# Part B's weights: three quarters of one Wo piece held in a PSUM bank, with three small banks and a new order of a segment

## The chip, the cores and the metric

The kernel runs on one core of a Trainium2 chip. The metric is the time of one execution on the device, in microseconds (us); a profile of one more execution comes with it. The engines that matter are TensorE (PE, matmuls; PEld its weight loads), VectorE (DVE), ScalarE (ACT), GpSimd (POOL), SyncE (SP, which issues most transfers) and the 16 DMA engines that carry them.

## What is computed

Two independent parts write the left and the right half of the output's columns. Part A is a sliding-window attention with dilation; the change does not touch it. Part B is a recurrent attention over segments of 32 rows with 8 memory rows that each segment hands to the next:

```python
for s in range(n_seg):                       # 64 segments of 32 rows, Dm = 640, H = 32, Dh = 192, M = 8
    h = jnp.concatenate([mem, xs], axis=1)   # 40 rows
    q = jnp.einsum('btd,dhe->bhte', h, Wq)   # Wq, Wk, Wv: 640 x 6144; Wo: 6144 x 640
    k = jnp.einsum('btd,dhe->bhte', h, Wk)
    v = jnp.einsum('btd,dhe->bhte', h, Wv)
    scores = jnp.where(mask, jnp.einsum('bhqe,bhke->bhqk', q, k) * scale, -1e9)
    o = jnp.einsum('bhqk,bhke->bhqe', softmax(scores), v)
    o = jnp.einsum('bhte,hed->btd', o, Wo)
    mem = o[:, :M, :]
    outs.append(o[:, M:, :])
```

So every segment needs all four weights, bf16, 7.9 MB each, and they do not all fit on the chip.

## The kernel before

**Pieces.** Wq, Wk and Wv are each cut into 4 groups g (eight heads) of 5 pieces dc, 128 x 1536 bf16 (384 KB); Wo into 24 pieces of 128 x 1280 (320 KB). Most pieces stay in SBUF (wres_...). Those in STREAMED (line 285) are copied to DRAM in a packed form (wcopy_...) while part A runs, and are fetched anew in every segment: 8 of Wk, 10 of Wv and 5 of Wo (8, 12, 17, 19, 23). `fetch` (line 472) takes a buffer of a ring of seven (`wstream`, tile t) and issues the load on SP (line 475). SP runs ahead of PE as far as the ring allows: a fetch waits until PE has finished with the piece that held the buffer seven pieces earlier.

**A segment** is a list of steps, ORDER (line 298; FIRST for segment 0), which fixes the order of the instructions on PE, DVE, ACT and SP. `q.g`, `k.g`, `v.g` are the projections of a group (line 562): 20 matmuls for the 24 new and 8 memory rows, and 20 more where the group's late rows are computed anew (RENEW: one group of k and one of v in each segment). The "late" rows are the last 8 rows of a segment, whose projections were made up to four segments ahead. `e.` copies a projection out of PSUM (line 601, or 568 for the late rows) and `T.` turns it in blocks on DVE (line 572); the tiles QT and KT are single, so the copy for the next group waits until the scores `S.` (line 626) have read them. Softmax is `sb`, `mx`, `sub`, `send` (lines 632 to 658), in place in the PSUM bank of the scores, with the exponential on ACT. `tp` (line 665) turns the probabilities on PE and `PT` (lines 673, 676) spreads them; `ve` copies the values (lines 615, 617); `mix` (line 689) multiplies probabilities and values in two banks, and `ot` copies the result (line 697) to the single tile OT. `out.g.half` (line 714) multiplies OT with Wo in the bank Y; `part` and `join` (lines 721, 726) add Y's halves; `last` (line 740) does the last six pieces of Wo, and `close` (lines 748, 749) writes the memory rows of the next segment to HX and the output rows to XS. `ql` projects late rows of the next segment's q. EVACUATE, HEADS and SPREAD say which of ACT (S) and DVE (V) does a copy.

**Rows in and out.** XS holds a segment's output rows after `close`. SP stores them in four transfers (line 772), one at each step of STORE_AT, and loads the next segment's x into the same tile after `ve.2` (line 535); `tx` turns it. The load waits for the stores.

**PSUM** has eight banks: three for projections (`ps_acc`), four small ones for S, tp, mix and last (`ps_x`, tile px) and Y (`ps_y`). A new px tile takes a bank whose last user is done.

**Around the segments.** Part A runs for the first 171 us or so, with the packed copies, the resident weights and the copies of x beside it. Then the first seven fetches go out, the rest of the resident weights follow, and segment 0 begins. After segment 63, `project_late` multiplies the late rows of all segments with Wo once more, in eight sums in PSUM.

Of the kernel before, what the change touches and what calls it, by code (L numbers as in the profile page):

```python
# [7 lines left out]
FP32 = mybir.dt.float32  # L8
BF16 = mybir.dt.bfloat16
ALU = mybir.AluOpType  # L10
# [13 lines left out]
def part_a(ctx, tc, A_x, A_wqkv, A_wo, out, ident, emit_loads):  # L24
# [241 lines left out]
    with tc.manual_schedule(engines={mybir.EngineType.PE, mybir.EngineType.DVE, mybir.EngineType.Activation}):  # L266
# [4 lines left out]
        for b in range(-1, n_blk):  # L271
# [10 lines left out]

STREAMED = {"q": ((), (), (), ()), "k": ((1, 3), (1, 2), (0, 2), (1, 3)), "v": ((0, 1, 4), (2, 4), (0, 2, 4), (0, 2)),
            "o": (8, 12, 17, 19, 23)}
PARTS = {}
SLOT = 1536
RENEW = {0: ("k0", "v2"), 1: ("k1", "v3"), 2: ("k2", "v0"), 3: ("k3", "v1")}
BLOCKS = 16  # L290
FIRST = """
    q.0 e.q0 T.q0 k.0 e.k0 T.k0 q.1 S.0 sb.0 e.q1 T.q1 k.1 mx.0 sub.0 e.k1 T.k1 send.0 v.0 ve.0 S.1 sb.1
    q.2 e.q2 tp.0 PT.0 T.q2 k.2 e.k2 T.k2 mx.1 sub.1 mix.0 ot.0 v.1 ve.1 send.1 S.2 sb.2 out.0.0 out.0.1
    tp.1 mx.2 sub.2 PT.1 q.3 e.q3 T.q3 k.3 send.2 e.k3 T.k3 mix.1 ot.1 v.2 ve.2 tp.2 PT.2 out.1.0 S.3
    sb.3 mx.3 sub.3 out.1.1 mix.2 ot.2 send.3 v.3 ve.3 out.2.0 tp.3 PT.3 tx out.2.1 part mix.3 ot.3 join
    ql eql last close Tql
# [12 lines left out]
LEAD_IN = 114  # L309
HEAD = 10  # L310

# [8 lines left out]
def part_b(ctx, tc, B_x, B_mem0, B_Wq, B_Wk, B_Wv, B_Wo, out, ident, n_seg, pre, nbuf, mid):  # L320
# [7 lines left out]
    wo_v = B_Wo.rearrange("h e d -> (h e) d").rearrange("(i k p) d -> p i k d", p=128, k=2)  # L328

    def streamed(u):  # L330
        return u[1] in STREAMED["o"] if u[0] == "o" else u[2] in STREAMED[u[0]][u[1]]

    def pieces(m, g):
# [14 lines left out]
    def quarter_cols(u):  # L348
        return 320 if u[0] == "o" else 384
# [11 lines left out]
    def quarter(w, u, i):  # L361

        n = quarter_cols(u)
        if isinstance(w, tuple):
            now = PARTS[u]
            v = w[0][:, n * i:n * i + n] if i < now else w[1][:, n * (i - now):n * (i - now) + n]
            return v.rearrange("p (b c) -> p b c", b=2) if u[0] == "o" else v
        if u[0] == "o":
            return w[:, 640 * (i // 2):640 * (i // 2) + 640].rearrange("p (b g c) -> p g b c", b=2, g=2)[:, i % 2]
        return w[:, n * i:n * i + n]  # L370

    def stream_cols(u):
        return quarter_cols(u) * PARTS.get(u, 4)

    def kept_cols(u):
        return quarter_cols(u) * (4 - PARTS[u]) if u in PARTS else unit_cols(u)
# [3 lines left out]
    def copy_streamed():  # L380

        for m, g in need:
            for u in pieces(m, g):
                if u in PARTS:
# [65 lines left out]
    def pool(name, **kw):  # L450
        return ctx.enter_context(tc.tile_pool(name=name, reuse_waits="tile", **kw))
# [10 lines left out]
    one = pool("b_one", bufs=1)  # L462
    small = pool("b_small", bufs=2)
    ps_acc = pool("b_ps_acc", bufs=3, space=PSUM)
    ps_x = pool("b_ps_x", bufs=4, space=PSUM)
    ps_y = pool("b_ps_y", bufs=1, space=PSUM)
    respool2 = pool("b_res2", bufs=1)
    place_resident(respool2, resident[n_pre + len(early):])
    wait.update(resident[n_pre + len(early):])

    fetched = {}

    def fetch(u):
        t = wstream.tile([128, SLOT], BF16, tag="ws")
        nc.sync.dma_start(t[:, 0:stream_cols(u)], copied[u])
        return t[:, 0:stream_cols(u)]

    pending = []
# [65 lines left out]
    def bank():  # L544
        return ps_x.tile([128, 512], FP32, tag="x", name="px")
# [212 lines left out]
    def segment(s):  # L758
# [10 lines left out]
        def step(name, *at):  # L769
# [75 lines left out]
    def project_late():  # L845
# [140 lines left out]
```

## Time and profile before

| | |
|---|---|
| median of 3 executions | 1868.72 us (1862.43 to 1874.19) |
| the profiled execution's own time | 1872.4 us |
| its span, first to last instruction | 1870.6 us |
| start of segment 0 on PE | 173.3 us |
| end of segment 0's last operation, line 749 | 211.3 us |
| that of segment 63 | 1805.8 us |
| granted TensorE clock, mean | 0.99 |

The page gives for each engine its busy time, share of the span and number of instructions, then the span in 40 equal slices, where a digit is a busy share in tenths. The DMA row is the mean busy share of the 16 DMA engines, the GB/s row what they moved. A row of the waits reads: engine and line that waited, what released it, us in total, times, the longest. A row by stretches gives the stretch, its length, the busy time of PE, PEld, DVE, ACT and POOL with their instruction counts, the granted clock, the DMA share and GB/s. In a row of instructions stand start, duration, engine, line, operation, output and inputs, count, and in brackets the idle time before it with what ended it. In a row of groups, the last part is total busy time, mean ns of one, and idle time before. "issue" is a wait that the profile does not explain.

### The profile page before, as it was taken

How to read it: one execution, taken by the hardware profiler on the slowest of the kernel's cores; microseconds unless marked ns; L12 is line 12 of the kernel's file. 1: busy time of each engine (PE TensorE's matmuls, PEld its weight loads, DVE VectorE, ACT ScalarE, POOL GpSimd, SP SyncE). 2: the span in 40 equal slices, each digit the busy share in tenths (PEclk: the TensorE clock that was granted, in tenths of full speed). 3: DMA queues.
4: the chain of work that ended last, by engine and by line, in shares of the span. 5: the costliest groups of instructions: out<-in, count | busy, mean ns of one | idle time of the engine just before them, and what ended most of it. 6: DMA issues, size and time to landing. Idle time of an engine off the chain costs nothing.

```text
span 1870.6 us, 91426 instructions
## 1 busy us (share of the span) xinstructions
PE 1651.0 (88%) x39286; PEld 1044.9 (56%) x39286; DVE 1289.4 (69%) x3671; ACT 683.2 (37%) x1821; POOL 548.6 (29%) x1612
## 2 busy tenths in 40 slices
PE   8898888888889888888888988888889888898888
PEld 5565555555555555555555555555555555555568
DVE  4786677667777776776777767777667777677740
ACT  3454333333333333333333333333333333333320
POOL 3001233233233233332333323323323333332320
PEclk9999999999999999999999999999999999999999
DMA  9926999999999999999999999999999999999991
GB/s 327 321 74 211 384 352 349 344 348 353 361 340 365 364 362 345 352 357 339 360 362 350 367 336 355 359 368 357 339 344 366 352 355 360 356 366 350 349 380 42
DMA packets 277859, 627.63 MB, mean 336 GB/s; under 512 B 64116, under 2 KB 76898, under 8 KB 277452
## 3 DMA queue, kind: packets, MB, share of 16 engines
q1 hardware_dynamic: 267020, 610.59, 91.4%
q0 software_dynamic: 10336, 11.12, 1.8%
q8 instruction: 308, 5.05, 1.1%
q14 instruction: 99, 0.81, 0.1%
q10 hardware_dynamic: 96, 0.06, 0.0%
HBM read 607.47 MB, written 22.91 MB: 337 GB/s over the span
## 4 chain that ended last, share of the span: by engine, by line
PE 48%; DMA 31%; DVE 10%; issue 5%; ACT 4%; SPq 1%; POOL 0%; ACTq 0%; DVEq 0%; POOLq 0%
PE acc L562 24%; DMA t<-wcopy_v 24%; PE Y L714 5%; DMA t<-wcopy_k 4%; PE px L626 3%; PE px L740 3%; PE pq L95 3%; PE px L689 3%; PE px L859 2%; DMA t<-wcopy_o 1%; PE po L161 1%; ACT OT L697 1%; ACT QT L721 1%; DVE OT L697 1%; PE px L665 1%
## 5 line engine op out<-in xcount | busy, mean ns | idle before, releaser
L562 PEld LDWEIGHTS <-HX 128*32 128x32 bf16 x19380 | 506.1, 97 | 385.7 <-issue 161.1
L562 PE MATMUL acc<-t,HX 128*32 128x384 bf16 x5812 | 433.8, 330 | 60.2 <-DMA t<-wcopy_v 38.8
L562 PE MATMUL acc<-wres_q,HX 128*32 128x384 bf16 x6460 | 327.5, 331 | 16.3 <-issue 14.7
L562 PE MATMUL acc<-wres_k,HX 128*32 128x384 bf16 x3876 | 269.7, 327 | 9.5 <-issue 8.4
L698 POOL COPY OL<-OT 128x96 bf16<-128x96 bf16 x256 | 158.9, 621 | 272.0 <-ACT OT L697 177.3
L562 PE MATMUL acc<-wres_v,HX 128*32 128x384 bf16 x3232 | 216.4, 330 | 5.1 <-issue 5.0
L697 DVE CAST OT<-px 128x240 bf16<-128x240 f32 x256 | 103.8, 405 | 164.0 <-PE px L689 148.4
L608 POOL COPY QT<-Lb 128x96 bf16<-128x96 bf16 x252 | 67.6, 268 | 479.2 <-PE px L626 478.9
L714 PE MATMUL Y<-wres_o,OT 128*32 128x320 bf16 x3840 | 189.9, 301 | 6.4 <-issue 6.4
L572 DVE STREAM_TRANSPOSE QT<-QT 128x384 bf16<-128x384 bf16 x256 | 146.6, 573 | 43.7 <-ACT QT L601 41.5
L697 ACT CAST OT<-px 128x240 bf16<-128x240 f32 x256 | 92.5, 361 | 222.9 <-PE px L689 131.3
L601 ACT CAST KT<-acc 128x384 bf16<-128x384 f32 x192 | 92.4, 481 | 223.1 <-PE px L626 174.0
L615 ACT CAST Vst<-acc 128x384 bf16<-128x384 f32 x256 | 123.5, 482 | 113.7 <-PE px L689 91.0
L626 PE MATMUL px<-KT,QT 64*64 64x40 bf16 (+1 forms) x4096 | 139.3, 189 | 28.2 <-DVE KT L572 20.6
L699 POOL DMA_DIRECT2D late_o<-OL x256 | 137.9, 539 | 77.0 <-POOL OL L698 60.5
L632 DVE SCALAR_TENSOR_TENSOR px<-px,mask 128x160 f32<-128x160 f32 x256 | 82.7, 323 | 108.3 <-PE px L626 107.7
L626 PEld LDWEIGHTS <-QT 64*64 64x64 bf16 (+1 forms) x4096 | 109.0, 109 | 86.2 <-issue 47.2
L714 PEld LDWEIGHTS <-OT 128*32 128x32 bf16 x4608 | 113.8, 96 | 58.5 <-issue 15.2
L572 DVE STREAM_TRANSPOSE KT<-KT 128x384 bf16<-128x384 bf16 x256 | 142.2, 556 | 3.1 <-ACT KT L601 1.5
L568 ACT CAST sb<-acc 128x384 bf16<-128x384 f32 x115 | 55.1, 479 | 232.7 <-PE acc L562 202.8
L644 ACT ACTIVATE px<-px 128x160 f32<-128x160 f32 x256 | 74.3, 290 | 145.1 <-DVE px L643 135.7
L689 PE MATMUL px<-PT,Vst 64*128 64x80 bf16 (+1 forms) x2048 | 122.6, 212 | 4.5 <-issue 2.5
(102 smaller groups left out, 2429.5 us busy)
## 6 DMA issues: line engine op xcount, KB each, us to landing
t<-wcopy_v SPq DMA_DIRECT2D x640, 384.0 KB, 5.9
t<-wcopy_k SPq DMA_DIRECT2D x512, 384.0 KB, 5.2
t<-wcopy_o SPq DMA_DIRECT2D x330, 320.0 KB, 6.0
wres_q<-in_B_Wq_dram SPq DMA_DIRECT2D x20, 384.0 KB, 8.0
late_o<-OL POOLq DMA_DIRECT2D x256, 24.0 KB, 5.2
wres_q<-late_o SPq DMA_DIRECT2D x16, 384.0 KB, 7.3
wres_o<-in_B_Wo_dram SPq DMA_DIRECT2D x19, 320.0 KB, 7.2
wres_k<-in_B_Wk_dram SPq DMA_DIRECT2D x12, 384.0 KB, 7.9
```

The lines of the kernel that those rows point to most:

```text
L562: nc.tensor.matmul(ps[n][32 * j:32 * j + 32].rearrange("p (f n) -> p f n", n=32), lhsT=X[:, dc, :], rhs=columns(w, (m, g, dc), j), start=( ...
L572: nc.vector.transpose(t, t)
L601: copies[1](columns_of(m, 0, 32), ps[-1][:].rearrange("p (f n) -> p f n", n=32))
L615: S_(Vst[:], ps[-1][:])
L626: nc.tensor.matmul(Sps[64 * h:64 * h + 64, a, :], lhsT=QT[k0:k1, L * f:L * f + 64], rhs=KT[k0:k1, f, :], start=(outer == 0 and a == 0), st ...
L632: nc.vector.scalar_tensor_tensor(out=Sps, in0=Sps, scalar=scale, in1=mask[:].unsqueeze(1).to_broadcast([128, 4, L]), op0=ALU.mult, op1=ALU ...
L644: nc.scalar.activation(t1[:], t1[:], ACTF.Exp)
L689: nc.tensor.matmul(ps[r][lo:hi, 2 * L * k:2 * L * k + 2 * L], lhsT=V[64 * r:64 * r + 64, col:col + hi - lo], rhs=PT[64 * r:64 * r + 64, 2 ...
L697: copy(OT[:, 6 * r:6 * r + 6].rearrange("p c n -> p (c n)"), ps[r][:, 0:6 * L])
L698: nc.gpsimd.tensor_copy(OL[:, g % 2].rearrange("p n c -> p c n"), OT[:, :, 32:L])
L699: nc.gpsimd.dma_start(late_o[s // 4][:, g, s % 4], OL[:, g % 2].rearrange("p n c -> p (n c)"))
L714: nc.tensor.matmul(Y[t:t + 32].rearrange("p (b c) -> p b c", b=2), lhsT=OT[:, slot(c), 0:32], rhs=quarter(w, ("o", i, 0), 2 * r + gv), sta ...
```

## The change

- STREAMED: in each segment 10 pieces of Wk, 8 of Wv and 4 whole ones of Wo are fetched.
- HELD: of piece 21 of Wo, three quarters (960 columns) are loaded once, at the start, and copied by DVE into a PSUM bank of their own (`hold`). The last quarter (320 columns, 640 bytes a partition) is packed in DRAM and fetched in each segment at the new step `w.0`; there ACT copies the 960 columns from PSUM into the same ring buffer beside it.
- `ps_x` has three banks in place of four. `project_late` takes its eighth sum from them after the first two blocks are stored.
- ORDER and FIRST are written anew. In ORDER, `send.1` stands ahead of `mix.0`, `k.2` between `S.0` and `S.1`, `out.1` ahead of `mix.2`, `v.3` behind `mix.2`, `w.0` between `tp.3` and `PT.3`.
- EVACUATE and HEADS: `e.q0` on ACT and `e.k3` on DVE for the current rows; both copies of `ot.2` on ACT.
- STORE_AT: the four stores are issued at `tp.0`, `mx.1`, `send.1` and `PT.0`, which puts two behind v.0's fetches and two behind v.1's. Five fetches stand between the last of them and the load of x, as before.

```diff
-STREAMED = {"q": ((), (), (), ()), "k": ((1, 3), (1, 2), (0, 2), (1, 3)), "v": ((0, 1, 4), (2, 4), (0, 2, 4), (0, 2)),
-            "o": (8, 12, 17, 19, 23)}
+STREAMED = {"q": ((), (), (), ()), "k": ((0, 3), (1, 2), (0, 2, 4), (1, 2, 4)), "v": ((0, 4), (3, 4), (1, 3), (2, 4)),
+            "o": (6, 11, 18, 22)}
+HELD = ("o", 21, 0)
...
 ORDER = """
-    q.0 e.q0 T.q0 k.0 k.1 e.k0 T.k0 q.1 S.0 sb.0 e.k1 e.q1 mx.0 sub.0 v.0 T.q1 ve.0 T.k1 q.2 S.1 send.0
-    e.q2 T.q2 sb.1 mx.1 k.2 tp.0 v.1 e.k2 q.3 PT.0 sub.1 mix.0 T.k2 send.1 tp.1 S.2 ve.1 ot.0 sb.2 e.q3
-    PT.1 mx.2 sub.2 k.3 T.q3 send.2 out.0.0 e.k3 v.2 out.0.1 mix.1 T.k3 S.3 ot.1 tp.2 sb.3 mx.3 v.3 PT.2
-    ve.2 mix.2 sub.3 out.1.0 send.3 out.1.1 ot.2 tp.3 ve.3 out.2.0 out.2.1 part tx PT.3 mix.3 ot.3 last
-    join ql close eql Tql
+    q.0 k.0 e.q0 T.q0 q.1 e.k0 T.k0 k.1 S.0 e.q1 sb.0 e.k1 T.q1 k.2 T.k1 mx.0 sub.0 S.1 e.k2 send.0 q.2
+    e.q2 sb.1 v.0 tp.0 mx.1 sub.1 ve.0 T.q2 v.1 send.1 T.k2 q.3 PT.0 mix.0 S.2 ve.1 ot.0 sb.2 e.q3 mx.2
+    tp.1 PT.1 k.3 mix.1 out.0.0 T.q3 v.2 out.0.1 e.k3 sub.2 T.k3 send.2 ot.1 ve.2 tp.2 S.3 PT.2 out.1.0
+    out.1.1 mix.2 sb.3 mx.3 sub.3 v.3 send.3 ot.2 tp.3 w.0 PT.3 out.2.0 out.2.1 ve.3 tx mix.3 part ot.3
+    join last ql close eql Tql
 """
-EVACUATE = {"k0": "SV", "k1": "SS", "k2": "VS", "k3": "SS", "q0": "VV", "q1": "SS", "q2": "SS", "q3": "VV"}
-HEADS = ("VS", "SV", "VS", "SV")
+EVACUATE = {"k0": "SV", "k1": "SS", "k2": "VS", "k3": "SV", "q0": "VS", "q1": "VS", "q2": "VS", "q3": "SV"}
+HEADS = ("VS", "SV", "SS", "SV")
-STORE_AT = ("tp.0", "PT.0", "tp.1", "e.k3")
+STORE_AT = ("tp.0", "mx.1", "send.1", "PT.0")
...
-    ps_x = pool("b_ps_x", bufs=4, space=PSUM)
+    ps_x = pool("b_ps_x", bufs=3, space=PSUM)
     ps_y = pool("b_ps_y", bufs=1, space=PSUM)
+    held = pool("b_ps_w", bufs=1, space=PSUM).tile([128, 512], FP32, name="held")
...
+    def hold():
+        t = wstream.tile([128, SLOT], BF16, tag="ws")
+        load_quarters(t[:, 0:960], HELD, (1, 2, 3))
+        nc.vector.tensor_scalar(out=held[:, 0:480].bitcast(mybir.dt.uint32), in0=t[:, 0:960].bitcast(mybir.dt.uint32),
+                                scalar1=0, scalar2=None, op0=ALU.bitwise_or)
+
     def fetch(u):
         t = wstream.tile([128, SLOT], BF16, tag="ws")
         nc.sync.dma_start(t[:, 0:stream_cols(u)], copied[u])
+        if u == HELD:
+            nc.scalar.copy(t[:, 320:1280], held[:, 0:480].bitcast(BF16))
+            return t[:, 0:1280]
...
+            elif name == "w":
+                fetched[HELD] = fetch(HELD)
...
-        sums = [bank()[:] for _ in range(4)] + [acc[0][:], acc[1][:], acc[2][:], y[:]]
+        sums = [bank()[:] for _ in range(3)] + [acc[0][:], acc[1][:], acc[2][:], y[:]]
...
+            else:
+                sums.append(bank()[:])
...
+    hold()
     fetch_first(nbuf)
```

FIRST gets `send.1` ahead of `mix.0`, `send.3` ahead of `mix.2` and `w.0` behind `tx`; the copies to DRAM take only the first quarter of the held piece.

More of the change, by code (lines that the diff above doesn't have):

```diff
@@ L292 @@
     q.0 e.q0 T.q0 k.0 e.k0 T.k0 q.1 S.0 sb.0 e.q1 T.q1 k.1 mx.0 sub.0 e.k1 T.k1 send.0 v.0 ve.0 S.1 sb.1
-    q.2 e.q2 tp.0 PT.0 T.q2 k.2 e.k2 T.k2 mx.1 sub.1 mix.0 ot.0 v.1 ve.1 send.1 S.2 sb.2 out.0.0 out.0.1
+    q.2 e.q2 tp.0 PT.0 T.q2 k.2 e.k2 T.k2 mx.1 sub.1 send.1 mix.0 ot.0 v.1 ve.1 S.2 sb.2 out.0.0 out.0.1
     tp.1 mx.2 sub.2 PT.1 q.3 e.q3 T.q3 k.3 send.2 e.k3 T.k3 mix.1 ot.1 v.2 ve.2 tp.2 PT.2 out.1.0 S.3
-    sb.3 mx.3 sub.3 out.1.1 mix.2 ot.2 send.3 v.3 ve.3 out.2.0 tp.3 PT.3 tx out.2.1 part mix.3 ot.3 join
-    ql eql last close Tql
+    sb.3 mx.3 sub.3 out.1.1 send.3 mix.2 ot.2 v.3 ve.3 out.2.0 tp.3 PT.3 tx w.0 out.2.1 part mix.3 ot.3
+    join ql eql last close Tql
 """
 ORDER = """
-    q.0 e.q0 T.q0 k.0 k.1 e.k0 T.k0 q.1 S.0 sb.0 e.k1 e.q1 mx.0 sub.0 v.0 T.q1 ve.0 T.k1 q.2 S.1 send.0
-    e.q2 T.q2 sb.1 mx.1 k.2 tp.0 v.1 e.k2 q.3 PT.0 sub.1 mix.0 T.k2 send.1 tp.1 S.2 ve.1 ot.0 sb.2 e.q3
-    PT.1 mx.2 sub.2 k.3 T.q3 send.2 out.0.0 e.k3 v.2 out.0.1 mix.1 T.k3 S.3 ot.1 tp.2 sb.3 mx.3 v.3 PT.2
-    ve.2 mix.2 sub.3 out.1.0 send.3 out.1.1 ot.2 tp.3 ve.3 out.2.0 out.2.1 part tx PT.3 mix.3 ot.3 last
-    join ql close eql Tql
-"""
-EVACUATE = {"k0": "SV", "k1": "SS", "k2": "VS", "k3": "SS", "q0": "VV", "q1": "SS", "q2": "SS", "q3": "VV"}
-HEADS = ("VS", "SV", "VS", "SV")
+    q.0 k.0 e.q0 T.q0 q.1 e.k0 T.k0 k.1 S.0 e.q1 sb.0 e.k1 T.q1 k.2 T.k1 mx.0 sub.0 S.1 e.k2 send.0 q.2
[3 more added lines that the diff above has]
+    join last ql close eql Tql
+"""
+EVACUATE = {"k0": "SV", "k1": "SS", "k2": "VS", "k3": "SV", "q0": "VS", "q1": "VS", "q2": "VS", "q3": "SV"}
+HEADS = ("VS", "SV", "SS", "SV")
 SPREAD = "SSVV"
-STORE_AT = ("tp.0", "PT.0", "tp.1", "e.k3")
+STORE_AT = ("tp.0", "mx.1", "send.1", "PT.0")
 LEAD_IN = 114
@@ L330, in streamed @@
     def streamed(u):
+        if u == HELD:
+            return True
         return u[1] in STREAMED["o"] if u[0] == "o" else u[2] in STREAMED[u[0]][u[1]]
@@ L363, in quarter @@
         n = quarter_cols(u)
+        if u == HELD:
+            return w[:, n * i:n * i + n].rearrange("p (b c) -> p b c", b=2)
         if isinstance(w, tuple):
@@ L372, in stream_cols @@
     def stream_cols(u):
-        return quarter_cols(u) * PARTS.get(u, 4)
+        return quarter_cols(u) * (1 if u == HELD else PARTS.get(u, 4))
     def kept_cols(u):
@@ L383, in copy_streamed @@
             for u in pieces(m, g):
-                if u in PARTS:
+                if u == HELD:
+                    copied[u] = dpool.tile([128, stream_cols(u)], BF16, name="wcopy_%s%d_%d" % u)[:]
+                    load_quarters(copied[u], u, (0,))
+                elif u in PARTS:
                     copied[u] = dpool.tile([128, stream_cols(u)], BF16, name="wcopy_%s%d_%d" % u)[:]
@@ L475, in fetch @@
         nc.sync.dma_start(t[:, 0:stream_cols(u)], copied[u])
+        if u == HELD:
+            nc.scalar.copy(t[:, 320:1280], held[:, 0:480].bitcast(BF16))
+            return t[:, 0:1280]
         return t[:, 0:stream_cols(u)]
```

## The prediction

> **What bounds the kernel now.** I read the page first, then the busy time by stretches, the DMA issues, the waits of TensorE and of the SP queue, and last one segment in order of time. From the page:
>
> ```profile
> span 1870.6 us, 91426 instructions
> PE 1651.0 (88%) x39286; PEld 1044.9 (56%) x39286; DVE 1289.4 (69%) x3671; ACT 683.2 (37%) x1821; POOL 548.6 (29%) x1612
> ...
> DMA  9926999999999999999999999999999999999991
> GB/s 327 321 74 211 384 352 349 344 348 353 361 340 365 364 362 345 352 357 339 360 362 350 367 336 355 359 368 357 339 344 366 352 355 360 356 366 350 349 380 42
> ...
> q1 hardware_dynamic: 267020, 610.59, 91.4%
> q0 software_dynamic: 10336, 11.12, 1.8%
> ...
> PE 48%; DMA 31%; DVE 10%; issue 5%; ACT 4%; SPq 1%; POOL 0%; ACTq 0%; DVEq 0%; POOLq 0%
> ```
>
> The mean over the span hides three stages. The last operation of a segment (line 749) marks the stage of the 64 segments, and the stretches give its load:
>
> ```profile
> L749 DVE TENSOR_TENSOR XS<-px,QT x64: 317/325/326, 211.3 to 1805.8; 128x160 bf16<-128x160 f32 x64
> ```
>
> ```profile
> core 0: us, PE busy (x) PEld busy (x) DVE busy (x) ACT busy (x) POOL busy (x), PEclk, DMA share, GB/s
> 211.31:1805.80 1594.49, 1409.89 (x35010) 874.58 (x35010) 1143.03 (x3477) 585.81 (x1621) 507.19 (x1509) 0.99 0.99 355
> ```
>
> 63 segments take 1594.49 us, 25.31 us each. The 16 DMA engines are busy for 0.99 of it at 355 GB/s, while PE is busy for 22.4 us of 25.31. The transfers set the pace; what PE lacks is in its waits:
>
> ```profile
> PEld L562 <- issue: 161.1, 282, 2.7
> ```
>
> ```profile
> PE acc L562 <- DMA t<-wcopy_v: 38.8, 78, 2.4
> PE px L740 <- ACT OT L697: 38.1, 63, 0.6
> ...
> PE px L626 <- DVE KT L572: 20.6, 35, 0.9
> ...
> PE acc L562 <- DMA t<-wcopy_k: 6.8, 17, 0.6
> ```
>
> Waits named for weights come to 45.6 us, 0.72 us a segment. So PE, freed of these, would need at most 25.31 - 0.72 = 24.59 us. The weight loads wait another 2.6 us a segment (161.1) for something that the profile doesn't name, which can be a landing too; if half of it is, PE's floor is nearer 23.3. The first place to look is thus which of the two floors, DMA's or PE's, is the higher after the change.
>
> **The change, part by part.** *Bytes.* Before, a segment streams these:
>
> ```profile
> t<-wcopy_v SPq DMA_DIRECT2D x640, 384.0 KB, 5.9
> t<-wcopy_k SPq DMA_DIRECT2D x512, 384.0 KB, 5.2
> t<-wcopy_o SPq DMA_DIRECT2D x330, 320.0 KB, 6.0
> ```
>
> That is 10 pieces of Wv, 8 of Wk, 5 of Wo: 8512 KB. After, it is 8 of Wv, 10 of Wk, 4 of Wo and a quarter piece of 80 KB: 8272 KB. 240 KB, 245,760 bytes, go; the count of transfers stays at 23 beside one load of x and four stores. At 355 GB/s this is 0.69 us. But the quarter has rows of 640 bytes. The two queues of the page give the cost of a packet: q0's 1.8% of 16 x 1870.6 us over 10,336 packets is 52 ns at 1076 bytes, q1's 91.4% over 267,020 is 102 ns at 2287 bytes; so about 7 ns and 0.0416 ns a byte, 114 ns for 2560 bytes and 34 ns for 640. 128 packets on 16 engines are eight each: 0.91 us becomes 0.27 us, **0.64 us a segment**, 41 us over 64. Bounds: 0.69 us if bytes alone count, zero if a small packet costs as much as a large one. I take 0.64, since the queue with packets of 1076 bytes stands nearest.
>
> The Trainium skill, page "DMA: Bandwidth & Descriptors", section "Bandwidth", speaks against this part: transfers under 64 KB are dominated by descriptors, and 64 KB take 0.95 us alone. Taken as engine time (an estimate), an 80 KB piece would cost about what the 320 KB one costs now, and the sum would come out at no gain. The 52 and 102 ns above speak for cost by size in a full queue.
>
> *The copy by ScalarE.* It moves 960 columns once a segment (line 492 of the changed kernel), after both copies of ot.2 and ahead of ve.3, part and ot.3. Its price, from
>
> ```profile
> L697 ACT CAST OT<-px 128x240 bf16<-128x240 f32 x256 | 92.5, 361 | 222.9 <-PE px L689 131.3 <-PE Y L714 90.0
> L615 ACT CAST Vst<-acc 128x384 bf16<-128x384 f32 x256 | 123.5, 482 | 113.7 <-PE px L689 91.0 <-PE acc L562 22.5
> L147 ACT CAST Pr<-pr 128x512 bf16<-128x512 f32 x32 | 17.2, 589 | 0.6 <-PE pr L145 0.6
> ```
>
> is 361 + 720 x 0.84 = 0.96 us (240 to 512 columns add 228 ns), at least 0.59 by the nearest row. ACT goes from 9.3 to 10.6 us a segment with one more copy of OT (HEADS), so it is no bound. What counts is the place: v.3 now runs after mix.2, so v.3, copy, ve.3 and mix.3 form a chain. While the copy runs PE has only tp.3 and out.2, and ve.3 comes 0.96 us later than it could. I estimate that half of this shows, 0.5 us of PE idle before mix.3, between none and all of the 0.96. The copy also waits for its piece, which lands 0.27 us after v3's last one, that PE needs anyway.
>
> *Three small banks and the order.* With S, tp and mix on three banks, mix.0 needs send.1 done, and tp.1 needs the first copy of ot.0; both are written ahead in the order. The place that costs is S.1. Before:
>
> ```profile
> 1003.36 0.54 PE L626 MATMUL px<-KT,QT 64*64 64x40 bf16 x16
> 1003.83 0.51 PE L562 MATMUL acc<-t,HX 128*32 128x384 bf16 x8
> ...
> 1004.65 0.99 PE L562 MATMUL acc<-wres_q,HX 128*32 128x384 bf16 x20
> ...
> 1006.08 0.54 PE L626 MATMUL px<-KT,QT 64*64 64x40 bf16 x16 [0.45 <-DVE KT L572]
> ```
>
> QT and KT are single tiles, so e.q1 and e.k1 wait for S.0, then each is turned: two copies and two turns, 2.72 us from S.0 to S.1, with v.0 (0.82 us) and q.2 (0.82) as cover. After, only k.2 (0.82; 1.64 where its late rows are renewed, one segment in four) stands between. One cover less is 0.82 us; against it, mx.0 and sub.0 now follow T.k1 on DVE instead of preceding it. I price it at 0.5 us net, from 0 to 0.8. send.2, now behind T.k3, holds up tp.2; at 0.2 us this is a guess, from 0 to the 0.5 of S.1. With the copy that is 1.2 us of new PE waits a segment.
>
> What covers them is PE's slack. DMA will need 25.31 - 0.64 = 24.67 us; PE 24.59 + 1.2 = 25.8 if only the named waits were weights, 23.3 + 1.2 = 24.5 if half of the unnamed ones were too. I stand by the second: in the chain of waits DMA holds 31% of the span, 9 us a segment, far more than 0.72, and the share is 0.99 throughout. With floors at 24.67 and 24.5 not every wait is covered, and I charge 0.16 us a segment, 10 us.
>
> At the end of a segment nothing changes: last still waits for ot.3 behind part.
>
> *Stores.* Before, they stand behind 9, 11, 11 and 13 pieces, the load of x five pieces after the last; after, behind 9, 9, 11, 11, with the load again five pieces on.
>
> ```profile
> SPq L772 <- DMA t<-wcopy_k: 30.8, 54, 1.0
> SPq L535 <- DMA out_dram<-XS: 29.2, 45, 1.7
> ```
>
> SP waits 60 us here in all, behind which the next fetches queue, but with five pieces in flight (5.9 us to landing) the engines stay fed. I cost the move at nothing; it may give or take a quarter of the 60 us, 15.
>
> *The start.* hold() puts three small loads ahead, and the seventh fetch must wait for its DVE copy, which needs part A's last bank (free after the copy of the second row below, 171 us). Six of the loads of resident weights, issued from 158 us on before, then queue behind it. The engines are partly idle there now:
>
> ```profile
> 158.22 1.39 SPq L407 DMA_DIRECT2D wres_q<-in_B_Wq_dram  x3
> ...
> 170.64 0.37 ACT L164 CAST ao<-po 128x256 bf16<-128x256 f32 x1 [0.29 <-PE po L161]
> ```
>
> ```profile
> 170.00:175.00 5.00, 5.00 (x70) 3.27 (x68) 0.00 (x0) 2.43 (x6) 1.47 (x6) 1.00 0.39 149
> 175.00:180.00 5.00, 3.98 (x94) 2.46 (x88) 3.56 (x7) 0.76 (x2) 1.78 (x8) 1.00 0.62 191
> ```
>
> Six pieces are 6.5 us of work; 3.1 + 1.9 us of idle time take most of it. Cost 2 us, 0 to 6.
>
> **Sum** against the profiled 1872.4 us: - 41 + 10 + 2 = 1843.4. That execution lies 3.7 us above the median, 1868.72; on the median's scale it is 1839.7. I say 1840.
>
> **The rivals.** *PE takes over.* If a quarter of the unnamed waits were weights, PE's floor is 23.9 + 1.2 = 25.1 us a segment: 63 x 0.2 = 13 us gained, about 1860. For it speaks that the floors are so close; against it, that the trace has PE waits of 0.6 us a segment (L740) that DMA's 0.99 does not feel.
>
> *The small piece is no cheaper.* Then the bytes bring nothing, DMA stays at 25.3 us a segment, and with the start it is about 1874. The packet costs above speak against it.
>
> *Slower: the copy blocks ScalarE.* It stands in order; if its quarter lands late, ve.3, part and ot.3, and with them mix.3, last and the next segment's memory rows, wait behind it. With PE's floor at 23.3 it decides from 25.31 - 23.3 = 2.0 us of new waits a segment, so 0.8 beyond the 1.2; a landing 1.5 us late makes 0.7 more, 63 x 0.7 = 44 us, about 1913. For it: DMA has no spare time, so landings are just in time. Against: SP issues this piece directly behind v.3's, and v.3 must wait for those.
>
> **How the numbers follow.** DMA-bound as summed: 0.60. PE takes over 0.17, small piece no cheaper 0.06: together within 1%, 0.23. The copy blocks: 0.17. About 1% is what a measurement here can tell from no change, so faster means under 1850 and slower over 1887. The range: below, 1840 less 15 for the stores, 10 for no PE charge and 3 for bytes alone, 1812; above, both cases of no change and the first part of the slower one, 1888. The likeliest case's own range is 1822 to 1850.
>
> **What would show it.** Right: the stage near 24.85 us a segment, DMA share still 0.97 or more, wcopy_o 4 full pieces and one of 80 KB a segment, an ACT copy near 0.96 us x64, PE's wait for DVE KT before S.1 up from 20.6 to about 50 us. Wrong: DMA share under 0.95 means that PE or ACT has taken over; an ACT copy that waits for its landing, with PE idle before L707 (mix), means the slower rival; share 0.99 at less than 350 GB/s means that the small packets are dear.

## The result and the profile after

The changed kernel takes 1890.82 us (median of 4 executions, 1885.37 to 1896.64), the kernel before 1865.58 us beside it (1856.61 to 1874.19). The ratio of the runs is 1.012, with a 95% interval of 1.0079 to 1.016 (the two medians alone are 25 us apart, 1.35%): slower by 1.2%, where 1840 us was predicted and 1888 was the range's upper end.

These are the page's rows of the changed kernel, whose profiled execution took 1885.37 us:

```profile
span 1883.4 us, 91543 instructions
PE 1644.8 (87%) x39286; PEld 1037.0 (55%) x39286; DVE 1276.9 (68%) x3609; ACT 763.4 (41%) x1950; POOL 556.6 (30%) x1612
...
DMA  9925999999999999999999999999999999999991
GB/s 328 311 70 212 373 347 325 348 338 356 343 335 357 341 325 348 342 348 337 338 344 357 346 338 351 336 344 355 333 338 352 330 324 348 347 344 333 334 370 42
...
q1 hardware_dynamic: 267836, 594.37, 89.9%
...
PE 52%; DMA 31%; DVE 8%; ACT 4%; issue 4%; SPq 0%; POOL 0%; DVEq 0%; ACTq 0%; POOLq 0%
```

The bytes went as the diff says, from 610.59 to 594.37 MB on the queue of SP. The digits of the DMA row are nines as before; the GB/s row is lower in most slices. The chain that ended last still holds 31% of DMA, and more of PE (52% against 48%). The stretch of the 64 segments, between the first and the last output row of close, shows it in one row:

```profile
213.20:1819.40 1606.20, 1405.16 (x35009) 867.08 (x35009) 1129.64 (x3414) 664.14 (x1748) 515.16 (x1509) 0.99 0.97 342
```

63 segments take 1606.20 us, 25.50 each, where before it was 25.31. The bytes of this stretch fell by 2.8% (8512 to 8272 KB of weights a segment), the rate by 3.7%, from 355 to 342 GB/s, and the busy share only from 0.99 to 0.97. The start cost 1.9 us (213.2 against 211.3). The pieces land as quickly as before, the small one hardly sooner than one of four times its size:

```profile
t<-wcopy_k SPq DMA_DIRECT2D x640, 384.0 KB, 4.9
t<-wcopy_v SPq DMA_DIRECT2D x512, 384.0 KB, 6.1
t<-wcopy_o SPq DMA_DIRECT2D x264, 320.0 KB, 5.5
...
t<-wcopy_o SPq DMA_DIRECT2D x66, 80.0 KB, 5.2
```

What PE waits for (line 580 is a projection, 644 the scores, 758 last):

```profile
PEld L580 <- issue: 180.1, 298, 2.3
...
PE acc L580 <- DMA t<-wcopy_k: 44.7, 76, 1.8
PE px L758 <- ACT OT L715: 39.4, 63, 0.6
...
PE acc L580 <- DMA t<-wcopy_v: 29.9, 60, 2.2
...
PE px L644 <- DVE KT L590: 23.4, 36, 0.8
```

The waits named for weights of k and v rose from 45.6 to 74.6 us, all of it by Wk (6.8 to 44.7, while Wv's fell from 38.8 to 29.9), and the unnamed ones of the projections from 161.1 to 180.1. The wait before S.1, which was to rise from 20.6 to about 50, is 23.4. ScalarE's copy has the length that was worked out (64 in the segments and two behind them):

```profile
L492 ACT COPY t<-held 128x960 bf16<-128x960 bf16 x66 | 65.1, 986 | 18.8 <-PE acc L879 18.8
```

So two things were left to explain: why 240 KB fewer in each segment did not shorten it, and what made it longer.

### The profile page after: what moved, and what is told of

Its sections match the earlier page's. It is cut to its first block, busy times and chain, and to the rows that moved or that the text cites. A ratio compares the mean times of both kernels' runs of the same rounds, so it can differ in the third digit from the quotient of the medians.

```text
span 1883.4 us, 91543 instructions
## 1 busy us (share of the span) xinstructions
PE 1644.8 (87%) x39286; PEld 1037.0 (55%) x39286; DVE 1276.9 (68%) x3609; ACT 763.4 (41%) x1950; POOL 556.6 (30%) x1612
## 3 DMA queue, kind: packets, MB, share of 16 engines
q1 hardware_dynamic: 267836, 594.37, 89.9%
## 4 chain that ended last, share of the span: by engine, by line
PE 52%; DMA 31%; DVE 8%; ACT 4%; issue 4%; SPq 0%; POOL 0%; DVEq 0%; ACTq 0%; POOLq 0%
PE acc L580 27%; DMA t<-wcopy_v 15%; DMA t<-wcopy_k 13%; PE Y L732 6%; PE px L644 4%; PE px L758 3%; PE pq L95 3%; PE px L683 2%; PE px L707 2%; ACT QT L739 1%; PE px L879 1%; PE po L161 1%; ACT QT L619 1%; ACT OT L715 1%; PE acc L879 1%
## 5 line engine op out<-in xcount | busy, mean ns | idle before, releaser
L580 PEld LDWEIGHTS <-HX 128*32 128x32 bf16 x19380 | 503.8, 97 | 419.3 <-issue 180.1
L580 PE MATMUL acc<-t,HX 128*32 128x384 bf16 x5816 | 426.1, 330 | 100.1 <-DMA t<-wcopy_k 44.7
L580 PE MATMUL acc<-wres_q,HX 128*32 128x384 bf16 x6460 | 318.2, 327 | 7.3 <-issue 6.1
L580 PE MATMUL acc<-wres_v,HX 128*32 128x384 bf16 x3876 | 244.5, 332 | 4.2 <-issue 4.2
L580 PE MATMUL acc<-wres_k,HX 128*32 128x384 bf16 x3228 | 228.3, 327 | 3.3 <-issue 2.6
L619 ACT CAST QT<-acc 128x384 bf16<-128x384 f32 x192 | 91.9, 479 | 230.6 <-PE px L644 170.9
L715 DVE CAST OT<-px 128x240 bf16<-128x240 f32 x192 | 78.1, 407 | 133.6 <-PE px L707 84.2
L644 PE MATMUL px<-KT,QT 64*64 64x40 bf16 (+1 forms) x4096 | 138.2, 189 | 28.1 <-DVE KT L590 23.4
L732 PEld LDWEIGHTS <-OT 128*32 128x32 bf16 x4608 | 108.9, 97 | 46.7 <-issue 10.1
L715 ACT CAST OT<-px 128x240 bf16<-128x240 f32 x320 | 109.7, 365 | 14.2 <-PE px L707 9.3
```

The lines of the kernel that those rows point to most:

```text
L580: nc.tensor.matmul(ps[n][32 * j:32 * j + 32].rearrange("p (f n) -> p f n", n=32), lhsT=X[:, dc, :], rhs=columns(w, (m, g, dc), j), start=( ...
L619: copies[1](columns_of(m, 0, 32), ps[-1][:].rearrange("p (f n) -> p f n", n=32))
L644: nc.tensor.matmul(Sps[64 * h:64 * h + 64, a, :], lhsT=QT[k0:k1, L * f:L * f + 64], rhs=KT[k0:k1, f, :], start=(outer == 0 and a == 0), st ...
L715: copy(OT[:, 6 * r:6 * r + 6].rearrange("p c n -> p (c n)"), ps[r][:, 0:6 * L])
L732: nc.tensor.matmul(Y[t:t + 32].rearrange("p (b c) -> p b c", b=2), lhsT=OT[:, slot(c), 0:32], rhs=quarter(w, ("o", i, 0), 2 * r + gv), sta ...
```

## The experiments

Four theories were set against each other. The first is the prediction's: the DMA engines are full, and bytes are time. The second: the number of pieces under way in the ring is the limit, so a small piece takes up the place of a large one. The third: the order, the set of streamed pieces and the banks cost by themselves. The fourth: ScalarE's copy makes the values late. All ratios are to the kernel before, run beside on the same chip.

**Bytes and the ring.** In the kernel before, one piece was cut to a quarter, without held bank, copy or new order:

```diff
+SMALL = (('o', 17, 0),)
...
-        return quarter_cols(u) * PARTS.get(u, 4)
+        return quarter_cols(u) * (1 if u in SMALL else PARTS.get(u, 4))
```

> The kernel before with one edit: of piece 17 of Wo only the first quarter (80 KB, 640 bytes a partition) is fetched in a segment, and it stands in for the other three (that part of the computation is changed). Order, banks, copies, stores and the count of 23 transfers stay. Theory DMA (the busy time of the DMA engines sets the pace, as predicted): 0.64 us a segment less, 41 us in all, ratio to before 0.978. Theory RING (what counts is how many pieces are in flight in the ring of seven; a small one holds a buffer as long as a large one): no gain, 0.995 to 1.005. Theories ORDER (the new order and three banks make PE wait) and COPY (ScalarE's copy makes ve.3 and mix.3 late) say nothing against DMA here: 0.978.

1854.68 us, 0.991 (0.9875 to 0.9944). The stretch of its segments:

```profile
211.30:1778.30 1567.00, 1400.02 (x35009) 870.10 (x35009) 1142.00 (x3477) 584.45 (x1621) 507.64 (x1509) 0.99 0.99 351
```

That is 24.87 us a segment in the profiled execution, one of the two fastest of seven, 0.44 less than before; 0.64 was predicted. By the ratio it is 17 us of the 41 (by its interval 10 to 23), by the medians 14. So the bytes are worth something, but only a part of it, by the ratio less than half, reaches the time. The whole piece was then left out, its place in the ring too:

```diff
+DROPPED = ("o", 17, 0)
...
     def get_unit(u):
+        if u == ("o", 17, 0):
+            u = ("o", 16, 0)
```

> The kernel before with piece 17 of Wo not fetched at all (16 stands in): 22 transfers a segment and 320 KB less. With a quarter of it left, 23 transfers and 240 KB less, it was 0.991. If bytes count: 0.987 to 0.990. If the place of a piece in the ring counts, which a small piece takes as long as a large one: 0.975 to 0.983.

1855.08 us, 0.9932 (0.9906 to 0.9958): above both of its branches and no better than with the quarter left in. A place in the ring is thus not what the small piece costs, and 80 KB more brought nothing that intervals of 0.3% can show. The ring itself, with six and with eight buffers:

```diff
-    part_b(..., pre=110000, nbuf=7,
+    part_b(..., pre=110000, nbuf=6,
```

> The kernel before with six buffers in the ring in place of seven, nothing else. Theory DMA: engines that are busy for 0.99 of the time are fed by six as by seven, 1.000 to 1.005. Theory RING: one seventh less in flight, slower by 2% or more, and the landing times go down (from 5.9 us towards 5) while PE's waits for weights go up.

```diff
+SHARED = {("o", 20, 0): ("o", 18, 0), ("o", 21, 0): ("o", 22, 0)}
...
-    part_b(..., pre=110000, nbuf=7,
+    part_b(..., pre=110000, nbuf=8,
```

> The kernel before with eight ring buffers in place of seven; for the room, pieces 20 and 21 of Wo are not loaded, pieces 18 and 22 stand in for them (so those columns of the output differ). Same transfers, same bytes, same matmuls a segment. Six buffers took 1.031 of before. Ring theory (the number of pieces in flight sets the rate): 0.975 to 0.990. DMA theory (the engines are full at a share of 0.99): 0.995 to 1.003, no change.

Six: 1928.88 us, 1.0313 (1.0277 to 1.035). Eight: 1867.43 us, 0.9996 (0.9964 to 1.0028). Fewer than seven hurts, more than seven brings nothing, so the second theory falls as the cause here. That the eighth buffer changes nothing is what the first theory expected, too; what comes next decides against that one. The page of the run with six buffers has another lesson, in two rows:

```profile
span 1937.7 us, 91424 instructions
...
q1 hardware_dynamic: 267020, 610.59, 90.2%
```

It moves the very packets of before, 267,020 and 610.59 MB, but they occupied the engines for 90.2% of 1937.7 us, 1748 us; before it was 91.4% of 1870.6, 1710 us. The busy time of the queue isn't the price of its bytes: it grows with the span.

**What each side needs alone.** If transfers set the pace, taking work from PE changes nothing:

```diff
-        for dc in range(5)[part]:
+        for dc in ((0, 4) if m == "q" else range(5)[part]):
```

> The kernel before with two of five matmul rounds in each projection of Wq (the scores then come from part of q), 2.4 us of PE less a segment; all transfers as before. If the DMA engines set the pace at 25.3 us a segment, as the prediction had it: 0.993 to 1.000. If PE's chain and the landings hold each other up: 0.95 to 0.985. A fall to 0.91 would be PE's time alone.

1816.31 us, 0.9713 (0.9668 to 0.9757). Its page and its stretch of segments:

```profile
span 1811.5 us, 83674 instructions
...
q1 hardware_dynamic: 267020, 610.59, 92.6%
```

```profile
211.00:1746.90 1535.90, 1277.80 (x31241) 765.64 (x31241) 1140.09 (x3477) 585.96 (x1621) 507.20 (x1510) 0.99 1.00 368
```

All transfers are there, PE is busy for 2.10 us a segment less, and a segment takes 24.38 us, 0.93 less. The engines that seemed full at 355 GB/s carry 368, and the same packets occupy them for 1677 us. That they merely run faster where PE is idle is not what the traces show: in steps of half a microsecond in which PE is busy for over 95%, the rate is 352 GB/s in the kernel before and 366 in this run; in steps in which it is busy for less than half, 365 and 373. So the transfers alone need at most 24.38 us. For the other side, 12 of the 23 streamed pieces were not fetched, and resident pieces stood in, in both kernels:

```diff
+STAND_IN = {("k", 0, 3): ("k", 0, 4), ..., ("o", 17, 0): ("o", 16, 0), ("o", 23, 0): ("o", 22, 0)}
...
     def get_unit(u):
+        u = STAND_IN.get(u, u)
```

> The kernel before without 12 of its 23 streamed pieces a segment: resident pieces of the same group stand in for them, so those parts of the projections differ. PE's matmuls, the order, the copies and the stores are unchanged, and the transfers fall to about half. It measures the time that PE, VectorE and ScalarE need by themselves. The prediction's 23.3 us a segment gives 0.933 of before, the upper bound of 24.59 gives 0.976. If the work on the chip and not the transfers sets the pace: 0.985 or more.

> The changed kernel without 12 of its 23 streamed pieces a segment, resident pieces standing in; the step w.0 with the small piece and ScalarE's copy stays. The prediction's floor of 24.5 us a segment gives 0.973 of before, 1.2 us a segment above the other floor run, or 0.04 of the time. If three banks and the order cost little by themselves and only fit the landings worse: 0.01 or less above the other floor run. If the order itself is the bound: 1.000 or more.

Before: 1734.73 us, 0.9282 (0.9239 to 0.9324). Changed: 1746.04 us, 0.934 (0.9301 to 0.9379). The stretches and the one wait that matters, of the kernel before with half of its transfers:

```profile
206.00:1670.50 1464.50, 1357.83 (x35016) 864.03 (x35020) 1132.82 (x3478) 584.72 (x1621) 509.76 (x1511) 1.00 0.62 191
```

```profile
PEld L564 <- issue: 19.0, 41, 1.6
```

and of the changed kernel:

```profile
210.30:1688.20 1477.90, 1359.36 (x35016) 855.13 (x35020) 1126.51 (x3414) 664.14 (x1749) 518.02 (x1511) 0.99 0.59 179
```

On-chip work needs 23.25 us a segment before and 23.46 after. Three banks, the copy, the order and its new waits thus cost at most 0.21 us a segment where nothing is late: the profiled executions are the fastest of the one kernel and the slowest of the other, and of the 11 us between the medians (0.6% of the time) some 4 lie ahead of the first segment's end. The unnamed wait of the projections fell from 161.1 to 19.0 us: nearly all of it was a wait for weights that the profile doesn't name. Not all of that time was won, as the unnamed waits of the scores and of mix grew by 15 us each (47.2 to 62.5, 45.8 to 60.5).

Neither side alone accounts for 25.31 us: 23.25 for the work on the chip, at most 24.38 for the transfers. The rest appears only with both. That they hold each other up (a piece is late, PE waits, the buffers come free later, the next pieces start later) fits these runs and this row of the kernel before, by which fetches wait on SP for PE's projections to free a buffer:

```profile
SPq L475 <- PE acc L562: 511.9, 643, 11.5
```

But this loop is argued, not shown: six buffers made the kernel slower, as it demands, yet an eighth, which should loosen it, brought nothing. The excess over the on-chip floor is 2.06 us before and 25.50 - 23.46 = 2.04 after, although 2.8% of the bytes are gone.

**The parts of the change, one at a time.** First the new order alone in the kernel before, all of ORDER (without w.0), FIRST, EVACUATE, HEADS and STORE_AT as in the change:

```diff
 ORDER = """
-    q.0 e.q0 T.q0 k.0 k.1 e.k0 T.k0 q.1 S.0 sb.0 e.k1 e.q1 mx.0 sub.0 v.0 T.q1 ve.0 T.k1 q.2 S.1 send.0
+    q.0 k.0 e.q0 T.q0 q.1 e.k0 T.k0 k.1 S.0 e.q1 sb.0 e.k1 T.q1 k.2 T.k1 mx.0 sub.0 S.1 e.k2 send.0 q.2
...
-STORE_AT = ("tp.0", "PT.0", "tp.1", "e.k3")
+STORE_AT = ("tp.0", "mx.1", "send.1", "PT.0")
```

> The kernel before with only the changed kernel's order of a segment, its first segment, its assignment of copies to ScalarE and VectorE and its places for the four stores; the streamed pieces (10 of Wv, 8 of Wk, 5 of Wo, all whole), four small banks and all bytes as before. The run with all of the new pieces but whole ones and four banks was 1.014 of before. If the order of the steps is what costs: 1.010 to 1.020 again. If it is the new set of streamed pieces (10 of Wk, 8 of Wv): 0.997 to 1.004.

1876.6 us, 1.005 (1.0022 to 1.0079): a cost, but less than the 1.010 that the order was to have at the least. Then the new set of streamed pieces alone, all whole:

```diff
-            "k": ((1, 3), (1, 2), (0, 2), (1, 3)), "v": ((0, 1, 4), (2, 4), (0, 2, 4), (0, 2)), "o": (8, 12, 17, 19, 23)
+            "k": ((0, 3), (1, 2), (0, 2, 4), (1, 2, 4)), "v": ((0, 4), (3, 4), (1, 3), (2, 4)), "o": (6, 11, 18, 21, 22)
```

> The kernel before with only the changed kernel's set of streamed pieces, all whole (10 of Wk, 8 of Wv, 5 of Wo: 6, 11, 18, 21, 22); order, copies, stores, banks and bytes as before. If the set of pieces costs: 1.008 to 1.018. If the order costs: 0.995 to 1.004. Both above 1.01 would mean that order and pieces fit neither of them with the other's.

1892.67 us, 1.0126 (1.008 to 1.0173). The same number of pieces, the same bytes and the same order as before, and slower. Both together, piece 21 whole, with four small banks and with three:

```diff
-            "o": (6, 11, 18, 22)}
-HELD = ("o", 21, 0)
+            "o": (6, 11, 18, 21, 22)}
+WHOLE = ("o", 21, 0)
...
-    ps_x = pool("b_ps_x", bufs=3, space=PSUM)
+    ps_x = pool("b_ps_x", bufs=4, space=PSUM)
```

> The changed kernel without the held piece: piece 21 of Wo is streamed whole, at the place of w.0, there is no copy by ScalarE, and the freed bank goes back to the small banks (four). Pieces, order, copies' engines and stores are those of the change; bytes are those of before (8512 KB a segment). Theory DMA alone: 1.000 to before. Theory ORDER: the order costs what the change lost plus the gain of the bytes, 25 + 41 us, ratio 1.03 or more. Theory COPY: 1.00. Theory RING: the count of transfers is as in the change, so near the change without the copy, 1.00 to 1.012.

> The changed kernel with piece 21 of Wo fetched whole and no copy, as in the run with four small banks (1.014), but with three: the count of banks alone. The floor runs put all that the change adds on the chip at 0.006 of the time, so: 1.012 to 1.018. If three banks are a cost of their own where transfers are late: 1.020 or more.

Four banks: 1896.37 us, 1.014 (1.0101 to 1.0178), which lies in none of the ranges named for the four theories. Three: 1894.17 us, 1.0151 (1.0114 to 1.0189). The bank that was given up costs nothing that can be measured. Then the held piece without ScalarE's copy (the first quarter stands in for the other three):

```diff
         if u == HELD:
-            return w[:, n * i:n * i + n].rearrange("p (b c) -> p b c", b=2)
+            return w[:, 0:n].rearrange("p (b c) -> p b c", b=2)
...
         if u == HELD:
-            nc.scalar.copy(t[:, 320:1280], held[:, 0:480].bitcast(BF16))
             return t[:, 0:1280]
```

> The changed kernel with ScalarE's copy left out: the quarter fetched stands in for the other three of piece 21 (that part of the computation is changed). Everything else stays, the held bank too. Theory COPY: back to 0.98, the predicted gain. Theory ORDER, RING: as the change, 1.005 to 1.015 to before, as PE idle before mix.3 costs little. Theory DMA: as predicted, 0.98.

1887.11 us, 1.0092 (1.0062 to 1.0123), far from the 0.98 that the fourth theory needs: the copy is not the loss. The runs make a chain from before to after, each with one more part:

| one part more | ratio to before | step |
|---|---|---|
| new order, old set of pieces | 1.005 | +0.5% |
| new set of pieces, all whole, four banks | 1.014 | +0.9% |
| three banks | 1.0151 | +0.1% |
| a quarter of piece 21 in place of the whole | 1.0092 | -0.6% |
| the copy: the changed kernel | 1.012 | +0.3% |

Each ratio is uncertain by 0.3 to 0.4%, so the steps of 0.1 and 0.3% can't be told from nothing; the copy's interval (1.0062 to 1.0123) overlaps that of the whole change. The sizes also depend on what was there before: with the new set in place, the new order adds 0.1% (1.0126 to 1.014) and not 0.5%. What makes the kernel slower is the set of pieces and, less, the order; the saved bytes then give back some 11 us. That the set is the larger part was tried from the other side, the changed kernel with the set of before:

```diff
-            "k": ((0, 3), (1, 2), (0, 2, 4), (1, 2, 4)), "v": ((0, 4), (3, 4), (1, 3), (2, 4)), "o": (6, 11, 18, 22)
-HELD = ("o", 21, 0)
+            "k": ((1, 3), (1, 2), (0, 2), (1, 3)), "v": ((0, 1, 4), (2, 4), (0, 2, 4), (0, 2)), "o": (8, 12, 19, 23)
+HELD = ("o", 17, 0)
```

> The changed kernel with the whole set of streamed pieces of before (10 of Wv, 8 of Wk, Wo 8, 12, 19, 23 whole and 17 held); order, banks, copy and bytes as changed. From the runs so far: order with the old set 1.005, less 0.009 for the bytes, plus 0.003 for the copy: 0.996 to 1.002 if the parts add up and the set of pieces was the main loss. If three small banks cost more than the floor runs show: 1.006 to 1.014.

1873.85 us, 1.0025 (0.9998 to 1.0052): all of the change but its set of pieces, and the loss of 1.2% is nearly gone. The waits for weights of this run, and of the changed kernel with everything whole and four banks:

```profile
PE acc L580 <- DMA t<-wcopy_v: 33.5, 64, 1.9
...
PE acc L580 <- DMA t<-wcopy_k: 2.0, 6, 0.4
```

```profile
PE acc L580 <- DMA t<-wcopy_k: 48.8, 77, 2.0
...
PE acc L580 <- DMA t<-wcopy_v: 28.1, 62, 1.6
```

In the new order PE hardly waits for Wk with the old set (2.0 us), and with the new one 48.8, or 44.7 with the held piece. (In the old order the new set shows as a wait for Wv, 51.8, beside 14.7 for Wk.) Which pieces of the set? First the five of Wo, put back to their old places, with the new sets of Wk and Wv:

```diff
-            "o": (6, 11, 18, 22)}
-HELD = ("o", 21, 0)
+            "o": (8, 12, 19, 23)}
+HELD = ("o", 17, 0)
```

> The changed kernel with the streamed Wo pieces of before: 8, 12, 19 and 23 whole and 17 held, in place of 6, 11, 18, 22 and 21; Wk, Wv, order, banks, copy and bytes as changed. In the changed kernel no streamed piece is used between v.3 and the last step, so no buffer comes free there, and the rate falls to about 300 GB/s in the last 4 us of a segment. If that gap is what the set of pieces costs: 0.996 to 1.005, and the last quarter of a segment above 330 GB/s. If the sets of Wk and Wv cost: 1.008 to 1.014, as the changed kernel (1.012).

1895.63 us, 1.0153 (1.0119 to 1.0187). Not Wo: the loss that those pieces were to be is still there. k.3 has three streamed pieces in the new set and two in the old, and from tp.1 to mix.1, between which it stands, the changed kernel needs 2.03 us in the mean over its segments, that with the old set 1.36. This row of the changed kernel is the last round of such a k.3, straight before mix.1 (in brackets the idle time and what ended it):

```profile
1016.83 0.35 PE L580 MATMUL acc<-t,HX 128*32 128x384 bf16 x4 [0.44 <-DMA t<-wcopy_k]
```

So one piece was moved out of k.3 into v.2, and, as a control, the other one out of k.2 into v.0:

```diff
-"k": ((0, 3), (1, 2), (0, 2, 4), (1, 2, 4)), "v": ((0, 4), (3, 4), (1, 3), (2, 4))
+"k": ((0, 3), (1, 2), (0, 2, 4), (1, 3)), "v": ((0, 4), (3, 4), (0, 2, 4), (2, 4))
```

> The changed kernel with one streamed piece moved: Wk's group 3 has two (1, 3) in place of three, Wv's group 2 three (0, 2, 4) in place of two; all else and all bytes as changed. The runs with three pieces in k.3 show PE waiting 36 to 52 us for wcopy_k and 2.0 to 2.2 us from tp.1 to mix.1, between which k.3 stands; those with two pieces show 2 to 4 us and 1.4 to 1.5. If that place is the loss: 1.001 to 1.006, wcopy_k wait under 12 us. If any split of 10 and 8 costs the same: 1.009 to 1.014.

```diff
-"k": ((0, 3), (1, 2), (0, 2, 4), (1, 2, 4)), "v": ((0, 4), (3, 4), (1, 3), (2, 4))
+"k": ((0, 3), (1, 2), (0, 2), (1, 2, 4)), "v": ((0, 1, 4), (3, 4), (1, 3), (2, 4))
```

> The control: the changed kernel with the other piece moved, Wk's group 2 with two (0, 2) in place of three and Wv's group 0 with three (0, 1, 4) in place of two; k.3 keeps its three. If k.3 is the loss: 1.009 to 1.014, with the wait for wcopy_k above 30 us. If the count of Wk's pieces is the loss wherever they stand: 1.003 to 1.008, as the other run.

k.3 relieved: 1887.25 us, 1.0084 (1.0046 to 1.0122). k.2 relieved: 1890.99 us, 1.0114 (1.0089 to 1.0139). Their waits for weights, in this order:

```profile
PE acc L580 <- DMA t<-wcopy_v: 53.2, 105, 2.2
...
PE acc L580 <- DMA t<-wcopy_k: 19.4, 36, 1.8
```

```profile
PE acc L580 <- DMA t<-wcopy_v: 28.8, 62, 1.9
...
PE acc L580 <- DMA t<-wcopy_k: 22.3, 45, 1.6
```

Neither run fits one of its branches whole. Where k.3 was relieved, tp.1 to mix.1 took 1.46 us in place of 2.03, but the wait for Wk fell from 44.7 to 19.4 and that for Wv rose from 29.9 to 53.2: it moved to another group, and most of the time did not come back. In the control both waits together fell from 74.6 to 51.1, and the time did not follow; so waits that are named for weights are no measure of the loss. Neither of these two pieces is the cause by itself. It is the sets of Wk and Wv as a whole, 18 pieces and the rounds in which they stand; which property of them decides is left open.

**The held piece in the order of before.** Two versions kept order, pieces and stores of before, with only the edits that three banks need. In the first, piece 19 is held and copied between ve.3 and part:

```diff
-... sub.1 mix.0 T.k2 send.1 tp.1 S.2 ve.1 ot.0 ... mix.2 sub.3 out.1.0 send.3 ... out.2.0 out.2.1
+... sub.1 send.1 mix.0 T.k2 tp.1 ot.0 S.2 ve.1 ... sub.3 out.1.0 send.3 mix.2 ... out.2.0 w.0 out.2.1
```

> The held piece in the order of before: piece 19 of Wo is held three quarters in a PSUM bank, its first quarter fetched in each segment at a step w.0 between out.2.0 and out.2.1 with ScalarE's copy; pieces 8, 12, 17 and 23 whole, those of Wk and Wv, the copies and the stores as before; three small banks, for which send.1 stands ahead of mix.0, ot.0 ahead of S.2 and send.3 ahead of mix.2. Bytes as in the changed kernel. If the changed kernel loses by its order alone and the bytes give what the run with a quarter of piece 17 gave (0.991): 0.990 to 0.998 with the copy. If three banks cost PE waits that no cover is left for: 1.000 to 1.010.

In the second, piece 8 is held, and w.0 stands behind v.2:

```diff
-HELD = ("o", 19, 0)
+HELD = ("o", 8, 0)
...
-    ... e.k3 v.2 out.0.1 ... out.2.0 w.0 out.2.1
+    ... e.k3 v.2 w.0 out.0.1 ... out.2.0 out.2.1
```

> As the run with the held piece in the order of before (1.014), but piece 8 of Wo is the held one and w.0 stands behind v.2, where ScalarE waits 2.4 us a segment for mix.1; 19 is whole again. In that run PE waited 66 us for OT before the last step, in before 38; that wait should be back near 38. If ScalarE's copy was what held it up: 0.995 to 1.003. If three banks are: 1.008 to 1.016.

Both expectations for the first put it too low: it takes 1894.81 us, 1.0142 (1.0096 to 1.0188). The second takes 1887.21 us, 1.0091 (1.0061 to 1.0121). PE's wait for ot.3 before last, in the first and in the second:

```profile
PE px L758 <- ACT OT L715: 66.1, 63, 1.4
```

```profile
PE px L758 <- ACT OT L715: 38.1, 63, 0.6
```

So ScalarE's copy does hold up last where it stands ahead of part and ot.3 (66.1 us against 38.1), as one of the rivals had feared for the change; the change avoids that (39.4). But the wait went back to 38, as expected, and the time did not go to the 0.995 to 1.003 that was to follow: in the old order something else costs as well. It falls where three banks were to put it, but three banks cost nothing in the new order, so that stays open. No version with a held piece was faster than the kernel before.

## Why the prediction was wrong, point by point

Two steps failed: that the transfers alone set the pace, so that bytes are time, and that the trade of streamed pieces costs nothing.

**What bounds the kernel.** This is the first of them: "The transfers set the pace", read from a share of 0.99. Taking 60% of the matmuls of q away, with the same transfers, gave 24.38 us a segment in place of 25.31. The share says that packets were open on the engines, not that no more could be carried: the same 610.59 MB occupied them for 1677, 1710 and 1748 us in three kernels. A place where the rate varies shows it too. Two stretches of one segment of the kernel before, then two of the changed kernel:

```profile
953.19:959.19 6.00, 5.85 (x142) 3.70 (x141) 4.69 (x15) 3.24 (x10) 0.46 (x2) 1.00 0.98 318
...
966.59:970.59 4.00, 3.46 (x90) 2.03 (x82) 2.69 (x11) 1.69 (x6) 1.73 (x4) 1.00 1.02 379
```

```profile
1058.65:1064.65 6.00, 6.00 (x153) 3.58 (x142) 5.19 (x18) 2.97 (x8) 1.09 (x5) 1.00 0.93 302
...
1072.05:1076.05 4.00, 3.52 (x86) 1.94 (x78) 2.62 (x10) 2.85 (x8) 1.82 (x4) 1.00 1.03 387
```

In the first pair the rate falls by 16% and the share by 4%, in the second by 22% and 10%. The GB/s row of the page before, 336 to 368 inside the segments, 384 and 380 in the slices at their two ends, had shown that 355 isn't what the engines can do.

**PE's floor** was right: 23.3 us predicted, 23.25 measured. That it fits so well is in part luck: it was made from half of the unnamed waits of the projections, of which nearly all went with half of the transfers (142 of 161 us), while other waits grew. But the prediction then took the higher of two floors as the time. Here the floors, 23.25 and at most 24.38, lie below 25.31, and both of them move the time: 0.93 us a segment for 2.10 us less of PE, 0.44 for 240 KB fewer.

**Bytes,** -41 us: the sign was right and the size too large. By itself the cut gave 0.991, -17 us; inside the changed kernel -0.6%, -11 us. The price of a packet, 7 ns and 0.0416 ns a byte, was made from busy shares, which the experiments show to hold waiting too. For 64 KB alone the Trainium skill (DMA: Bandwidth & Descriptors, section Bandwidth) gives 0.95 us; no run here shows a transfer alone. The prediction's estimate from it, by which a piece of 80 KB would cost about as much as one of 320 KB, would have given no gain; the 0.991 speaks against that estimate, though the landing of 5.2 us beside 5.5 shows that in this ring a small piece arrives hardly sooner.

**New waits of PE,** 1.2 us a segment, of which 0.16 uncovered, +10 us. The listed waits were too dear: with half of the transfers, all that the change adds on the chip is at most 0.21 us. The wait before S.1 is 23.4 us in all, not 50, and where half of the transfers are missing 35.8 beside 28.3 of the kernel before: it rises by 7 us and not by 30.

**The set of streamed pieces** is the second step that failed, and the term that was missing: order and set decide when each piece must have landed. The prediction counted pieces and bytes ("the count of transfers stays at 23") and priced the trade of two pieces of Wv for two of Wk at nothing, with no other reason. It costs 0.9 to 1.3%, 17 to 23 us; the order, with the stores' new places, 0.1 to 0.5%, 2 to 9 us.

**The copy** takes 0.986 us (0.96 predicted) and costs at most some 0.3%. **Stores:** not tried by themselves; they are within the order's 0.5%. **The start** cost 1.9 us, as worked out (2).

**The rivals.** None was it. PE did not take over: its floor is 23.46. Two of the rivals' times (1860, 1874) were made from the profiled 1872.4 us and not from the median, 4 us too high beside the rest. That ScalarE's copy blocks would have given the right sign, but without the copy the kernel is as slow within the intervals, and last did not wait longer for ot.3 (39.4 us, 38.1 before). The sign named for dear packets, a lower rate, did appear (342), but with everything whole the loss was no smaller (1.014), so small packets are not what it comes from.

Against 1867 us the steps of the chain are +9 for the order, +17 for the set, +2 for the bank, -11 for the bytes, +5 for the copy. They add up to the 22 us of the ratio 1.012 because they are differences of one chain of runs; that sum is no test of its own. The run with the old set is one (1.0025).

## What to carry to other kernels

Here a DMA share of 0.99 told that something was always under way, not that the engines were at their limit (355 GB/s at 0.99, 368 at 1.00 with less of PE). So look at whether the rate in GB/s varies, and take work from the other side (fewer matmuls, or half of the loads with stand-ins) before bytes are turned into time. Where loads and matmuls both lie within some per cent of the time, as here, each saving was worth a part of itself (0.93 of 2.10 us, 0.44 of 0.64), and which pieces are fetched counted as much as how many there are: a new set of streamed pieces has to be costed as a schedule, even at the same bytes. And what each side needs alone, a run with half of the loads shows where a chain of waits can't.

## What was not expected of the hardware

- In the changed kernel a 320 KB piece lands 5.5 us after its issue and one of 80 KB 5.2; in the kernel before with one piece cut, the small one took longer than the large ones. In the two kernels that hold a piece in the old order the small one took 3.9 and 7.2 us beside 5.6, so its place made more of a difference than its size:

```profile
t<-wcopy_o SPq DMA_DIRECT2D x264, 320.0 KB, 5.6
...
t<-wcopy_o SPq DMA_DIRECT2D x66, 80.0 KB, 6.5
```

- Six buffers cost 3.1%, an eighth brought nothing.
- Leaving 320 KB a segment out (0.9932) was worth no more than leaving out 240 KB (0.991). The intervals (0.9906 to 0.9958, 0.9875 to 0.9944) leave room for a small gain; whether it ends there is open.
